# Loops on ScalarE and GpSimd, a shorter loop on VectorE, and the last wo rows loaded in strips

## The chip, the core and the metric

The kernel runs on one core of a Trainium2 chip. The metric is device time in microseconds of one execution, as the median of several. One execution was also taken by the hardware profiler; all rows quoted below come from that one, and times inside it count from the first instruction of its span. A core has five engines with a queue of instructions each: TensorE (PE, matmuls), VectorE (DVE), ScalarE (ACT), GpSimd (POOL) and SyncE (SP, which here only starts transfers). They meet through semaphores. Transfers between HBM (the large memory) and SBUF (the on-chip memory) run on 16 DMA engines that all queues share.

## The reference

One decode step for a batch of two: attention with grouped heads over a long cache, an output projection, a small MLP block on the same layer-normed token, and a gated sum. Cut to what matters:

```python
B, Sq, D = 2, 1, 512
Hq, Hkv, Sk, Dh = 32, 8, 32768, 128
xn = layernorm(x)
q = (xn @ wq)                                   # [B, Hq, 1, Dh]
scores = einsum("bhqd,bhkd->bhqk", q, k) * Dh ** -0.5    # four query heads share one kv head
o = einsum("bhqk,bhkd->bhqd", softmax(scores), v)
s = o.reshape(B, Sq, Hq * Dh) @ wo              # wo is 4096 x 512
out = x + s * silu(mlp_block(xn))               # weights w1 .. w4, hidden width 1792
```

All inputs are bf16. Each of the 2 x 8 pairs of batch and kv head has a K and a V of 32768 x 128, 8 MB each, so the two caches are 268 MB. With S = 1 the shifts inside the MLP block leave nothing of w1 and w2, so the kernel loads w3 and w4 alone.

## The kernel before

There are 16 head groups (one batch entry and one kv head each). For a group, K lands in SBUF with 128 partitions of 64 KB (`kbuf`, three slots of half a K), and V the same (`vbuf`, one V). K is not in the layout that a score matmul wants, so DVE transposes it in 32 x 32 blocks, 16 transposes of 128 x 1024 words a group (L493), through four buffers `T`; PE multiplies them with a padded, head-selecting form of q called `z` (L562) into two PSUM banks `sc`, one for each half. DVE takes the maximum of each half (`peak`, L476), PE spreads it over the partitions (L574), DVE makes `shift` (L503), ACT takes exponentials `ep` with row sums `rs` (L417), DVE transposes these to `pt` (L511) and makes the denominators' input `sm` (L508), and PE multiplies `pt` with V into `o` (L584). ACT copies `o` to `ob` (L420). The rest of a group's head, `head_on` and `head_out` on DVE with `head_oT` and `head_xp` on PE, is worked off inside the next group's K stage; it ends in four columns `oXs`, which POOL copies into `oX` (L438). POOL also writes `z` for the next group (L427).

Order and queues. PE and DVE run loops (PE's body is one group, DVE's two). ACT and POOL have all 16 groups written out one after the other. Every DVE wait in the loop is an instruction of its own (`take`, L473: wait for a semaphore, then subtract), and the DVE loop carries a branch hint at the top of each pass (`hint_back_edge`, L482). SP starts nearly all transfers, in this order: wq, w3, w4, K of group 0, V of group 0 (once the MLP no longer needs `vbuf`), then in turn the next K, when PE reports that the first half of the present K has been used (`s_half`, L398), and the next V, when PE reports that the present V has been used (`s_pv`, L387). The last K and V go in halves (L404, L392). Behind them in the same queue come the seven parts of wo (`wo_parts`, L411): four kv heads at once (2 MB), three heads of 512 KB each, and the last head as 256, 128 and 128 KB, all with 128 partitions. ACT's queue starts the small loads: x, four strips of x into `x4_bf` (L270) and four copies of the MLP's gate g into `g4` (L379).

The end, `pe_output`: PE waits for each wo part (`d_wo`) and for the `oX` columns that go with it, multiplies (L608, L615), and after the last part DVE multiplies by the gate (L520) and adds x (L521), and SP and ACT store one batch row each (L523). PE then runs 24 further waits (`PAD`, L627) and two hinted branches. A semaphore of a transfer counts to 16.

Of the kernel before, what the change touches and what calls it, by code (L numbers as in the profile page):

```python
# [14 lines left out]
DVE = mybir.EngineType.DVE  # L15

KPT = 128
RT = 16
# [74 lines left out]

@with_exitstack
def kernel(
# [62 lines left out]
    rec = sb("rec", [128, rep], F32)  # L158
    on = sb("on", [128, NQ, rep], BF16)
# [4 lines left out]
    x4 = sb("x4", [128, QW], F32)  # L164
# [35 lines left out]
    oX = sb("oX", [128, Hkv, NQ, B], BF16)  # L200
# [11 lines left out]
    wo_parts = [(0, 4, 0, NQ), (4, 5, 0, NQ), (5, 6, 0, NQ), (6, 7, 0, NQ), (7, 8, 0, 2), (7, 8, 2, 3), (7, 8, 3, NQ)]  # L212
    KC = 2
    PAD = 24
# [18 lines left out]
    t_d = sem("t_d")  # L233
    t_k = [sem(f"t_k{i}") for i in range(NPART)]
    t_v = [sem(f"t_v{i}") for i in range(NPART)]
    s_half, s_pv, s_shift, s_oX = (sem(f"s_{n}") for n in ("half", "pv", "shift", "oX"))
# [13 lines left out]
    with tc.tile_critical(sync_engine=mybir.EngineType.Pool, no_gpsimd_drain=True):  # L250
# [5 lines left out]
        nc.sync.sem_inc(t_k[1], 16)  # L256
# [12 lines left out]
        for n in range(NQ):  # L269
            ac.op(lambda e, n=n: e.dma_start(out=x4_bf[32 * n:32 * n + B, :], in_=A_x[:, 0, n * QW:(n + 1) * QW]), e_x4z, inc=(d_x4, 16))  # L270
# [26 lines left out]
        with nc.allow_low_precision(reason="one of the terms is one, the others are zero"):  # L297
# [23 lines left out]
            out=sel_w[:, :, :], in_=row_of[:, :].unsqueeze(1).broadcast_to([128, 4, 32])), e_row)  # L321

# [55 lines left out]
        for n in range(NQ):  # L378
            ac.op(lambda v, n=n: v.dma_start(out=g4[32 * n:32 * n + B, :], in_=g[:, n * QW:(n + 1) * QW]), e_g, e_g0, inc=(d_g, 16))  # L379
        e_x4 = ve.op(lambda v: v.tensor_copy(out=x4[:, :], in_=x4_bf[:, :]), (d_x4, 16 * NQ))  # L380
        ve.op(lambda v: v.memset(qrb[:, :], 0.0), e_qr)
        e_s0 = ve.op(lambda v: v.memset(pro[:, :], 0.0))


        def load_v(m, *events):
            if m < NG - 1:
                sp.op(lambda e: e.dma_start(out=vbuf[:, :], in_=row_view(A_v_cache, *groups[m])), *events, inc=(t_v[0], 16))  # L387
                nc.sync.sem_inc(t_v[1], 16)
                return
            for h in range(NPART):  # L390
                c = slice(h * SLOT, (h + 1) * SLOT)
                sp.op(lambda e, c=c: e.dma_start(out=vbuf[:, c], in_=row_view(A_v_cache, *groups[m])[:, c]), *events, inc=(t_v[h], 16))  # L392

        load_v(0, e_h2)
        for m in range(1, NG):
            base = m % 2
            if m < NG - 1:
# [3 lines left out]
                nc.sync.sem_inc(t_k[1], 16)  # L401
# [7 lines left out]
        for i, (a, c, r0, r1) in enumerate(wo_parts):  # L409
            cols = slice(r0 * D, r1 * D)  # L410
            sp.op(lambda e, a=a, c=c, cols=cols: e.dma_start(out=wo3[:, a:c, cols], in_=wos[:, a:c, cols]), (s_pv, NG - 1), inc=(d_wo[i], 16))  # L411


        for m in range(NG):
            for h in range(NPART):
                i = order(m).index(h)
                ac.op(lambda v, i=i: v.activation(  # L417
                    out=ep[i][:, :], in_=sc[i][:, :], func=ACT.Exp, scale=inv_sqrt_dh, bias=shift[:, :], accum_out=rs[:, i:i + 1]),
                    (s_shift, m + 1), e_tf if m == 0 else None, inc=(t_e, 1))
            ac.op(lambda v: v.copy(out=ob[:, :], in_=o[:, :]), (s_pv, m + 1), inc=(t_ob, 1))  # L420

        z_cols = z[:, :, :, (NR - 1) * rep:].rearrange("p n e c -> p (n e) c")
        z_cols = z_cols[:, :, 0:128].rearrange("p w (j c) -> p w j c", j=4)[:, :, :, 0:rep]

        def put_z(m):
            b, k = groups[m]
            po.op(lambda v: v.tensor_mul(  # L427
                out=z_cols,
                in0=qr[:, :, :, b, k * rep:(k + 1) * rep].rearrange("p n e h -> p (n e) h").unsqueeze(2).broadcast_to([128, 2 * NB, 4, rep]),
                in1=quad[:, :].unsqueeze(1).unsqueeze(3).broadcast_to([128, 2 * NB, 4, rep])),  # L430
                e_qr, e_z0, e_quad, (s_shift, m) if m else None, inc=(t_z, 1))

        e_oX = [None] * NG
        put_z(0)
        for m in range(NG):
            if m:
                b, k = groups[m - 1]
                e_oX[m - 1] = po.op(lambda v, b=b, k=k: v.tensor_copy(out=oX[:, k, :, b], in_=oXs[:, :]), (s_oX, m + 1))  # L438
            if m < NG - 1:
                put_z(m + 1)  # L440


        def head_on(last=False):
            take(nc.vector, t_S)
            nc.vector.tensor_reduce(
                out=den[:, :], in_=S[:, 0:NPART * rep].rearrange("p (i h) -> p h i", h=rep),
                axis=AX.X, op=ALU.add).then_inc(t_d, 1)
            take(nc.vector, t_d)
            nc.vector.reciprocal(out=rec[:, :], in_=den[:, :]).then_inc(t_d, 1)
            take(nc.vector, t_d)  # L450
            nc.vector.tensor_mul(
                out=recm[:, :, :], in0=rec[:, :].unsqueeze(1).broadcast_to([128, NQ, rep]),
                in1=sel_h[:, :].unsqueeze(2).broadcast_to([128, NQ, rep])).then_inc(t_oT, 1)
            take(nc.vector, t_oT, 2)
            ins = nc.vector.tensor_mul(
                out=on[:, :, :], in0=oT[:, :].unsqueeze(1).broadcast_to([128, NQ, rep]), in1=recm[:, :, :])
            if last:
                ins.then_inc(t_on, 1)

        def head_out(last=False):  # L460
            take(nc.vector, t_xp)
            nc.vector.tensor_mul(
                out=xm[:, :, :], in0=xp_b[:, :].rearrange("p (r h) -> p r h", r=NQ),
                in1=mask[:, :].unsqueeze(1).broadcast_to([128, NQ, rep])).then_inc(t_d, 1)
            take(nc.vector, t_d)
            with nc.allow_low_precision(reason="three of the four terms are zero, the fourth is bf16"):
                if last:
                    b, k = groups[-1]
                    return ve.op(lambda v: v.tensor_reduce(out=oX[:, k, :, b], in_=xm[:, :, :], axis=AX.X, op=ALU.add))
                nc.vector.tensor_reduce(out=oXs[:, :], in_=xm[:, :, :], axis=AX.X, op=ALU.add).then_inc(s_oX, 1)  # L470
# [4 lines left out]
        def peak(i):  # L475
            nc.vector.tensor_reduce(out=mx[:, i:i + 1], in_=sc[i][:, :], axis=AX.X, op=ALU.max).then_inc(t_d, 1)  # L476
            take(nc.vector, t_d)
            ins = nc.vector.tensor_scalar_mul(out=mxr[:, i, :], in0=row_of[:, :], scalar1=mx[:, i:i + 1])  # L478
            if i == NPART - 1:
                ins.then_inc(t_mx, 1)  # L480

        with nc.Fori(0, NG // 2, engines=[DVE], hint_back_edge=True):  # L482
            for par in range(2):
                take(nc.vector, t_z)
                for i, h in enumerate(order(par)):
                    take(nc.vector, t_k[i], 16)
                    u = par + h
                    kt = kbuf[:, u * SLOT:(u + 1) * SLOT].bitcast(I32)
                    for r in range(NR):
                        n = i * NR + r  # L490
                        if n >= T_BUFS:
                            take(nc.vector, t_used)
                        nc.vector.transpose(  # L493
                            out=Ts[n % T_BUFS][:, :].rearrange("p (b t k) -> p t b k", b=NB, t=RT),
                            in_=kt[:, r * W:(r + 1) * W].rearrange("p (t b k) -> p t b k", b=NB, t=RT)).then_inc(t_T, 1)
                        if i == 1 and r == 3:
                            peak(0)
                            head_on()
                head_out()
                take(nc.vector, t_used, T_BUFS)  # L500
                peak(1)
                take(nc.vector, t_top)
                nc.vector.tensor_reduce(  # L503
                    out=shift[:, :], in_=S[:, NPART * rep:], axis=AX.X, op=ALU.min).then_inc(s_shift, 1)
                for h in range(NPART):
                    take(nc.vector, t_e)
                    if h == NPART - 1:
                        nc.vector.tensor_mul(  # L508
                            out=sm[:, :, :], in0=sel_h[:, :].unsqueeze(1).broadcast_to([128, NPART, rep]),
                            in1=rs[:, :].unsqueeze(2).broadcast_to([128, NPART, rep]))  # L510
                    nc.vector.transpose(  # L511
                        out=pt[h][:, :, :].rearrange("p r (t h) -> p t r h", h=rep),
                        in_=ep[order(par).index(h)][:, :].rearrange("p (t r h) -> p t r h", r=NR, h=rep)).then_inc(t_pt, 1)
        head_on(last=True)
        e_oX[NG - 1] = head_out(last=True)


        e_ws, e_s = (pe.sem, pe.n + 1), (pe.sem, pe.n + 2)
        e_wsum = ac.op(lambda v: v.copy(out=wsum, in_=qrb[:, :]), e_ws)
        e = ve.op(lambda v: v.tensor_tensor(out=sg[0:QP, :], in0=pro[0:QP, 0:QW], in1=g4[0:QP, :], op=ALU.mult), (d_g, 16 * NQ), e_s)  # L520
        e = ve.op(lambda v: v.tensor_tensor(out=out4[0:QP, :], in0=sg[0:QP, :], in1=x4[0:QP, :], op=ALU.add), e, e_x4)  # L521
        for b, q in ((0, sp), (1, ac)):
            q.op(lambda v, b=b: v.dma_start(out=out[b, 0, :].rearrange("(n c) -> n c", c=QW), in_=out4[b:QP:32, :]), e, inc=(d_out, 16))  # L523
        sp.wait((d_out, 32))


        def head_oT(marks=None):
            take(nc.tensor, t_ob)
            for t in range(VT):
                if t == VT - 1 and marks:  # L530
                    marks.append(nc.tensor.mark_branch_hint_location())
# [18 lines left out]
        with nc.body("pe_groups", valid_engines=[PE]):  # L550
# [39 lines left out]
            ins.then_inc(s_pv, 1)  # L590
# [7 lines left out]
        with nc.body("pe_output", valid_engines=[PE]):  # L598

            marks = [nc.tensor.mark_branch_hint_location()]  # L600
# [63 lines left out]
```

## Time and profile before

| what | value |
|---|---|
| median of 3 runs | 657.68 us (657.57 to 657.85) |
| profiled execution, its own time | 657.31 us |
| its span, first to last instruction | 655.5 us |
| PE, PE weight loads, DVE busy | 409.6, 164.1, 380.2 us |
| ACT, POOL busy | 39.5, 10.1 us |
| bytes moved, mean rate | 280.58 MB, 428 GB/s |
| mean granted clock of TensorE | 0.81 |

The page cuts the span into 40 slices and gives for each the busy share of every engine and of the 16 DMA engines in tenths. The queues are listed with their packets: q1 is what SP starts, q10 what ACT starts, and packets of the kind "instruction" are instruction code that is brought in while the program runs. The chain of waits follows the work that ended last back from the last instruction. A row of the waits names the waiting engine and line, the releaser, the sum in us, the count, and the longest. "DVEq" or "PEq" with L473 means that the engine's own sequencer stood in a `take`.

### The profile page before, as it was taken

The numbers are of one execution on the slowest core, as the hardware profiler recorded it, in microseconds if no ns is written. First come the engines' busy times: TensorE is split into PE (matmuls) and PEld (weight loads), VectorE is DVE, ScalarE is ACT, GpSimd is POOL, SyncE is SP. The second block draws the span as 40 slices with busy tenths as digits, with TensorE's granted clock in tenths as the row PEclk, the third lists the DMA queues.
The fourth block names the chain that finished last, engine by engine and source line by source line (L and its number), as shares of the span: only waits on it lengthen the run. The fifth ranks groups of instructions, "written<-read, shape, count | busy, mean of one in ns | idle before, by whom it ended". The sixth has DMA issues, their size and how long they took to land. (4 is left out here: it accounts for less than half of the span.)

```text
span 655.5 us, 6482 instructions
## 1 busy us (share of the span) xinstructions
PE 409.6 (62%) x2444; PEld 164.1 (25%) x2444; DVE 380.2 (58%) x534; ACT 39.5 (6%) x89; POOL 10.1 (2%) x43
## 2 busy tenths in 40 slices
PE   2528386564938656494765749566383856648765
PEld 0113132231313212131321313232131322213323
DVE  5348194673819457291855729285482937638770
ACT  1100101000010000001000000100001010000100
POOL 1000000000000000000000000000000000000000
PEclk9859677696987769697686969878696887979798
DMA  8999999999999999999999999999999999999996
GB/s 365 435 449 444 445 420 420 444 444 444 396 448 444 444 428 412 448 440 444 416 428 444 440 448 400 444 444 440 440 404 448 440 444 420 424 444 414 448 418 262
DMA packets 6779, 280.58 MB, mean 428 GB/s; under 512 B 746, under 2 KB 1012, under 8 KB 2036
## 3 DMA queue, kind: packets, MB, share of 16 engines
q1 hardware_dynamic: 6728, 280.50, 99.0%
q8 instruction: 2, 0.03, 0.0%
q14 instruction: 5, 0.04, 0.0%
q10 hardware_dynamic: 44, 0.01, 0.0%
HBM read 280.50 MB, written 0.00 MB: 428 GB/s over the span
## 5 line engine op out<-in xcount | busy, mean ns | idle before, releaser
L493 DVE STREAM_TRANSPOSE T<-kbuf 128x1024 int32<-128x1024 int32 x256 | 295.7, 1214 | 186.7 <-DVEq L473 186.4
L562 PE MATMUL sc<-T,z 128*128 128x512 bf16 x1024 | 280.2, 422 | 164.9 <-PEq L473 161.8
L562 PEld LDWEIGHTS sc<-T,z 128*128 128x128 bf16 x1024 | 98.8, 104 | 330.1 <-issue 251.7
L584 PE MATMUL o<-vbuf,pt 128*16 128x512 bf16 x1024 | 90.8, 533 | 35.0 <-PEq L473 35.0
L584 PEld LDWEIGHTS o<-vbuf,pt 128*16 128x16 bf16 x1024 | 34.3, 117 | 85.8 <-issue 78.4
L417 ACT ACTIVATE ep<-sc,shift 128x512 bf16<-128x512 f32 x32 | 21.7, 682 | 479.8 <-DVE shift L503 479.8
L511 DVE STREAM_TRANSPOSE pt<-ep 128x512 bf16<-128x512 bf16 x32 | 22.6, 708 | 15.3 <-DVEq L473 15.3
L476 DVE TENSOR_REDUCE mx<-sc 128x1 f32<-128x512 f32 x32 | 21.5, 672 | 15.7 <-DVEq L473 15.7
L574 PE MATMUL S<-mxr,same_h 128*128 128x64 f32 x32 | 6.5, 284 | 22.0 <-PEq L473 22.0
L532 PEld LDWEIGHTS oT<-sel_o,ob 128*128 128x128 f32 x136 | 17.7, 191 | 3.2 <-issue 0.5
L532 PE MATMUL oT<-sel_o,ob 128*128 128x4 f32 x136 | 16.2, 243 | 0.5 <-PEq L473 0.5
L420 ACT COPY ob<-o 128x512 f32<-128x512 f32 x16 | 9.4, 585 | 97.0 <-PE o L584 97.0
L574 PEld LDWEIGHTS S<-mxr,same_h 128*128 128x128 f32 x32 | 4.8, 188 | 29.8 <-issue 29.8
L438 POOL COPY oX<-oXs 128x4 bf16<-128x4 bf16 x15 | 2.8, 188 | 520.8 <-DVE oXs L470 520.8
L478 DVE TENSOR_SCALAR mxr<-row_of,mx 128x32 f32<-128x32 f32 x32 | 7.7, 241 | 4.8 <-DVEq L473 0.3
L503 DVE TENSOR_REDUCE shift<-S 128x1 f32<-128x64 f32 x16 | 3.6, 225 | 11.2 <-DVEq L473 11.2
L591 PEld LDWEIGHTS S<-sm,ones_f 128*128 128x128 f32 x32 | 4.8, 188 | 6.9 <-issue 6.9
L372 PE MATMUL sc<-vbuf,h_bf 128*2 128x512 bf16 x14 | 4.8, 521 | 2.4 <-DVE h_bf L369 2.4
L417 ACT ACTIVATION_READ_ACCUMULATOR ep<-sc,shift 128x1 f32 x32 | 6.3, 196 | 0.0
L427 POOL TENSOR_TENSOR z<-qr,quad 128x64 bf16<-128x64 bf16 x16 | 4.7, 292 | 102.2 <-DVE shift L503 86.4
L591 PE MATMUL S<-sm,ones_f 128*128 128x8 f32 x32 | 6.2, 266 | 0.0
L336 PE MATMUL sc<-kbuf,xT 128*2 128x512 bf16 x32 | 3.6, 627 | 4.1 <-DMA kbuf<-in_A_wq_dram 4.1
(88 smaller groups left out, 63.6 us busy)
## 6 DMA issues: line engine op xcount, KB each, us to landing
kbuf<-in_A_k_cache_dram SPq DMA_DIRECT2D x2, 4096.0 KB, 21.7
vbuf<-in_A_v_cache_dram SPq DMA_DIRECT2D x2, 4096.0 KB, 20.2
kbuf<-in_A_wq_dram SPq DMA_DIRECT2D x1, 4096.0 KB, 12.3
vbuf<-in_B_w_dram SPq DMA_DIRECT2D x2, 1792.0 KB, 18.0
kbuf<-in_A_wo_dram SPq DMA_DIRECT2D x1, 2048.0 KB, 29.3
kbuf<-in_A_wo_dram SPq DMA_DIRECT2D x3, 512.0 KB, 30.8
kbuf<-in_A_wo_dram SPq DMA_DIRECT2D x1, 256.0 KB, 31.7
kbuf<-in_A_wo_dram SPq DMA_DIRECT2D x2, 128.0 KB, 15.6
```

Source lines behind the costliest of these rows:

```text
L372: e_h2 = pe.op(lambda t, f=f: t.matmul(h2[0:B, :], lhsT=h_bf[:, f * B:(f + 1) * B], rhs=w4v[:, f, :], start=(f == 0), stop=(f == FK - 1)), ...
L417: ac.op(lambda v, i=i: v.activation(out=ep[i][:, :], in_=sc[i][:, :], func=ACT.Exp, scale=inv_sqrt_dh, bias=shift[:, :], accum_out=rs[:, i ...
L420: ac.op(lambda v: v.copy(out=ob[:, :], in_=o[:, :]), (s_pv, m + 1), inc=(t_ob, 1))
L476: nc.vector.tensor_reduce(out=mx[:, i:i + 1], in_=sc[i][:, :], axis=AX.X, op=ALU.max).then_inc(t_d, 1)
L478: ins = nc.vector.tensor_scalar_mul(out=mxr[:, i, :], in0=row_of[:, :], scalar1=mx[:, i:i + 1])
L493: nc.vector.transpose(out=Ts[n % T_BUFS][:, :].rearrange("p (b t k) -> p t b k", b=NB, t=RT), in_=kt[:, r * W:(r + 1) * W].rearrange("p (t ...
L511: nc.vector.transpose(out=pt[h][:, :, :].rearrange("p r (t h) -> p t r h", h=rep), in_=ep[order(par).index(h)][:, :].rearrange("p (t r h) ...
L532: ins = nc.tensor.matmul(oT[:, :], lhsT=ob[:, t * Dh:(t + 1) * Dh], rhs=sel_o[:, t, :], start=(t == 0), stop=(t == VT - 1))
L562: ins = nc.tensor.matmul(sc[i][:, :], lhsT=z[:, nb, w, zc:zc + 128], rhs=Tb[:, nb, :, w], start=(r == 0 and nb == 0 and w == 0), stop=(r = ...
L574: nc.tensor.matmul(S[:, NPART * rep:], lhsT=same_h[:, :], rhs=mxr[:, :, :].rearrange("p i r -> p (i r)"), start=True, stop=True).then_inc( ...
L584: ins = nc.tensor.matmul(o[32 * j:32 * j + VT * rep, :], lhsT=pt[h][:, r, a * VT * rep:(a + 1) * VT * rep], rhs=vt[:, u * VT:(u + 1) * VT, ...
L591: nc.tensor.matmul(S[:, 0:NPART * rep], lhsT=ones_f[:, :], rhs=sm[:, :, :].rearrange("p i h -> p (i h)"), start=True, stop=True).then_inc( ...
```

## The change

- ACT's and POOL's 16 groups become loops (ACT eight passes of two groups, POOL fifteen of one). ACT now waits for DVE's `shift` (`t_shift`) and PE's `o` (`t_pv`) in the loop, and it is ACT that passes "V used" on to SP (`s_pv`). POOL's next `z` waits for `sm` instead of `shift`. A dummy exponential (`warm`) stands ahead of ACT's loop.
- DVE's loop: semaphore waits ride on the instructions that need them and count up through a pass; the subtractions are done together at the end of a pass. The branch hint is placed once, in the prologue, instead of in each pass. In the built program DVE has 147 instructions instead of 192, ACT 40 instead of 80, SP 78 instead of 91, POOL 55 instead of 68.
- Of the seven wo parts the last two (128 KB each) are loaded in strips of 40, 40, 40 and 8 partitions, so SP starts 13 wo transfers instead of 7. Their semaphores count to 64.
- The loads of `x4_bf` and `g4` go to SP's queue; SP's 30 semaphore increments, one at each K and V, become two at the start; the f32 copy `x4` is gone.
- Alignment directives pad the code: DVE's last two operations to slots 126 and 127 of a block of 128 instructions, and what SP, ACT and POOL run after the stores to the start of such a block, PE's end to a block of 256. Padding is jumped over. PE's 24 idle waits are gone; its hinted branch stands ahead of the last wo part.

```diff
+    STRIPS = ((0, 40), (40, 80), (80, 120), (120, 128))
+    wo_rows = [((0, 128),)] * (len(wo_parts) - 2) + [STRIPS] * 2
...
-        nc.sync.sem_inc(t_k[1], 16)
+        nc.sync.sem_inc(t_k[1], 16 * (NG - 1))
+        nc.sync.sem_inc(t_v[1], 16 * (NG - 1))
...
-            ac.op(lambda e, n=n: e.dma_start(out=x4_bf[32 * n:32 * n + B, :], in_=A_x[:, 0, n * QW:(n + 1) * QW]), e_x4z, inc=(d_x4, 16))
+            sp.op(lambda e, n=n: e.dma_start(out=x4_bf[32 * n:32 * n + B, :], in_=A_x[:, 0, n * QW:(n + 1) * QW]), e_x4z, inc=(d_x4, 16))
...
+        hint_v = nc.vector.mark_branch_hint_location()
...
-            sp.op(lambda e, a=a, c=c, cols=cols: e.dma_start(out=wo3[:, a:c, cols], in_=wos[:, a:c, cols]), (s_pv, NG - 1), inc=(d_wo[i], 16))
-        for m in range(NG):
-            for h in range(NPART):
-                i = order(m).index(h)
-                ac.op(lambda v, i=i: v.activation(
-                    out=ep[i][:, :], in_=sc[i][:, :], func=ACT.Exp, scale=inv_sqrt_dh, bias=shift[:, :], accum_out=rs[:, i:i + 1]),
-                    (s_shift, m + 1), e_tf if m == 0 else None, inc=(t_e, 1))
-            ac.op(lambda v: v.copy(out=ob[:, :], in_=o[:, :]), (s_pv, m + 1), inc=(t_ob, 1))
+            for p0, p1 in wo_rows[i]:
+                sp.op(lambda e, a=a, c=c, cols=cols, p0=p0, p1=p1: e.dma_start(
+                    out=wo3[p0:p1, a:c, cols], in_=wos[p0:p1, a:c, cols]), (s_pv, NG - 1), inc=(d_wo[i], 16))
+        with nc.Fori(0, NG // 2, engines=[ACTE]):
+            for par in range(2):
+                take(nc.scalar, t_shift)
...
+                take(nc.scalar, t_pv)
+                nc.scalar.sem_inc(s_pv, 1)
+                nc.scalar.copy(out=ob[:, :], in_=o[:, :]).then_inc(t_ob, 1)
...
+        with nc.Fori(0, NG - 1, engines=[POOL]) as m:
+            put_o(m)
+            take(nc.gpsimd, t_sm)
+            put_z(m + 1)
...
-        with nc.Fori(0, NG // 2, engines=[DVE], hint_back_edge=True):
+        nc.br("dve_groups", engines=[DVE])
+        with nc.body("dve_groups", valid_engines=[DVE]):
+            c = Counts()
...
+            for s_, n in c.totals():
+                take(nc.vector, s_, n)
+            nc.regs_alu(turn_v, turn_v, 1, op=ALU.add)
+            nc.vector.br_lt(turn_v, NG // 2, on_true="dve_groups", on_false="dve_last").branch_hint(hint_v)
...
+        nc.vector.addr_align(128, offset=126, max_nops=0)
...
+            (nc.sync if q is sp else nc.scalar).addr_align(128, max_nops=0)
+        nc.gpsimd.addr_align(128, max_nops=0)
...
+                if i == len(wo_parts) - 2:
+                    nc.tensor.br_ne(turn, 0, "pe_end", "pe_groups").branch_hint(mark)
+                    nc.switch_bb("pe_end")
...
-            for _ in range(PAD):
-                nc.tensor.wait_ge(d_wo[-1], 16)
...
+            nc.tensor.addr_align(256, max_nops=0)
```

## The prediction, made before the result was known

> **What bounds the kernel.** I read the page first, then the waits, then the end of the chain.
>
> ```profile
> DMA  8999999999999999999999999999999999999996
> q1 hardware_dynamic: 6728, 280.50, 99.0%
> q8 instruction: 2, 0.03, 0.0%
> q14 instruction: 5, 0.04, 0.0%
> ```
>
> The DMA engines are full in every slice between the first and the last; SP's queue q1 alone holds them for 99% of the span. The first packet of the weights starts at 1.93 us, the last lands at 651.23, and spread over their durations the packets run at 434 GB/s throughout. A 64 KB packet takes 2418 ns on its engine, a 1 KB packet 46 ns. So only three stretches can move: 1.9 us ahead, the point at which the last of 16 DMA engines is done, and 4.3 us behind that.
>
> The waits, of all engines and then of SP's two kinds of issue, tell how far compute is from mattering:
>
> ```profile
> DVE T L493 <- DVEq L473: 186.4, 39, 12.3
> ACT ep L417 <- DVE shift L503: 479.8, 16, 31.8
> ```
>
> ```profile
> L387 SPq DMA_DIRECT2D vbuf<-in_A_v_cache_dram x15: 327/328/328, 29.2 to 575.7; - x15
> DMA to landing us min/median/max: 24.6/26.4/32.1
> ```
>
> DVE, the busiest engine next to PE, idles up to 12.3 us in one wait for K. A V load (8.39 MB at 434 GB/s: 19.3 us) lands 24.6 us or more after its issue. Less 19.3, the 1.04 us from the first issue (0.89) to its first packet, and 1.7 us by which the slowest DMA engine lands behind the first: 2.6 us in which the next load is queued but not yet needed. A group may grow by that before the stream stops.
>
> The end of the chain (start, us, what) and of the timeline:
>
> ```profile
> 638.62 12.61 DMA kbuf<-in_A_wo_dram
> ...
> 651.27 0.26 PE pro L615 x4
> ...
> 651.55 0.30 DVE sg L520
> ...
> 651.88 0.29 DVE out L521
> ```
>
> The last wo part lands, four matmuls and two DVE operations follow, and the stores go out at 652.19. Their landing at 654.13 and the closing barrier fill the rest.
>
> **Why some DMA engines are late.** Each of the 16 adds one to a transfer's semaphore, so the increments show them finishing. For the last wo part ten come between 649.59 and 649.93, three near 650.16, then 650.60, 651.14 and 651.23. The three late ones were made long before: after an instruction packet at 35.84 one engine falls back 0.85 us, after one at 71.86 (16 KB, q8) another 1.4, after 265.30 a third 0.6, after 638.05 a fourth 0.5, and they never catch up, since each engine has its own share of every load. Inside the window 649 to 652:
>
> ```profile
> q8 instruction: 1, 0.02, 2.0%
> q14 instruction: 1, 0.01, 0.6%
> ```
>
> Two more; the q14 packet at 650.54 puts 0.31 us on the second-latest engine (650.50 for the part before, 651.14 instead of 650.83). The trace does not name who asked for a packet. By time, 35.84 fits DVE entering its loop (31.8), 71.86 and 649.70 PE (the only 16 KB ones), 265.30 ACT, 638.05 POOL, 643.37 SP, 650.54 DVE leaving its loop.
>
> **Part by part.**
>
> *Loops on ACT and POOL, fewer SP instructions.* With half the code on ACT and 13 instructions less on POOL and SP, the packets at 265.30, 638.05 and 643.37 should go; their three engines (at most 650.60) were not last: 0 by itself, up to -0.1. New costs: the word "V used" passes through ACT, a wait and an increment. A DVE wait instruction delays the next operation by 0.11 us (57.13 to 57.24), so I take 0.2; the 2.6 us hide it. `z` waits for `sm`, 1.85 us later than `shift` (609.68 against 607.83), so the last `z` comes at 610.0 instead of 608.14; DVE's next transposes start at 612.24. ACT's branch runs in idle stretches of up to 31.8 us. At the end `ob` comes 0.2 later, so `oX` at 648.6 instead of 648.43; the part that needs it is multiplied at 650.63: hidden, and bare only if wo came 2 us sooner.
>
> *DVE's loop.* About 40 wait instructions a pass go, ten subtractions come at its end, 10 x 0.11 = 1.1 us beside the wait for K. 0 in the stream. The early hint may keep the packet at 35.84 away: its engine is the second-latest, so this matters only together with the latest.
>
> *x4 and g on SP.* Eight issues of 0.33 us each, ahead of V 0 (29.2) and between V 0 and K 1 (53.39), where SP waits over 20 us; they are read at 651.55. 0. On their two DMA engines 27 ns rows lie in line instead of on a second queue: 0 to -0.1.
>
> *Strips.* The two parts are 256 rows of 1 KB. Loads over 2 partitions show data packets on two engines, stores over 4 on four, loads over 128 on all 16: an even split over a divisor. For 40 partitions the largest up to 16 is 10 engines with 4 rows each; for 8 it is 8. Three strips of 40 and one of 8 give, for both parts, 26 rows on eight engines, 24 on two, none on six, instead of 16 everywhere. Ten engines gain 10 x 46 ns = 0.46 us and six semaphore packets of 9 ns (0.05); six lose 16 x 46 = 0.74. Ordinary engines then end at 650.1 to 650.45. The latest (0.96 to 1.4 us behind; I keep the q8 packet at 71.86, as PE's loop is unchanged) ends at 651.23 - 0.74 = 650.49 if it is one of the six, at 651.74 if one of the ten. Which engines the six are no row shows; I take the first, because nothing late is known of the two that carry x and g, and because the sizes fit (0.5 + 0.74 against 1.4). [...]
>
> *Issues.* Eight strips instead of two: 8 x 0.45 = 3.6 us from 638.6 on, when the queue takes them (before that it stalls SP for 13.4 and 6.3 us). They are issued by 642.3; wo part 4, ahead of them, lands from 648.9: 6 us of cover. [...]
>
> *Alignment.* Jumps on SP and ACT come after the stores have been issued, POOL's after `out4`: beside the 1.3 us in which SP waits for the stores. Between +2.8 (a late fetch, below) and -0.2 (no packet beside the stores); nearest is the covered case, 0.
>
> **Sum.** Last landing 650.5 instead of 651.23, the 4.3 us behind it unchanged: -0.7. Span 654.8, profiled time 656.6. The median shown is 0.37 above the profiled execution, so 657.68 - 0.7 = 657.0.
>
> **Rivals.**
> - *The latest engine is one of the ten.* Last landing 651.74: +0.5, 658.2. For it: ten of sixteen. Against: fewer late engines remain.
> - *The strips do nothing:* 40 partitions go over all 16, or the queue shares otherwise. Then only packets saved count: 651.23 stays, 657.7, or 657.3 if the packet at 71.86 moves. The 2- and 4-row transfers speak against it.
> - *Slower: the jump at the end lands in code that is not there.* SP's jump over the padding is the place. From DVE's loop entry (31.7) to its packet (35.84) are 4.1 us under load; if SP must wait that long, 1.3 are covered and 2.8 bare: 657.0 + 2.8 = 659.8. It decides once the fetch takes over 1.3 + 0.7 = 2.0 us. Idle DMA engines speak for 1.4 (1.04 issue to packet, 0.31 packet). [...] This trace's back edges show no packet between 71.86 and 638 but one, so the loops are held to be free here.
>
> **Chances.** The forecast 0.64 (656.3 to 657.4 mostly; 0.16 of it, with every packet gone and a shorter end, beats 656.4); latest engine among the ten 0.12; strips without effect 0.08; late fetch or another stall 0.16. A difference under 0.2% (1.3 us) is about what a measurement of this kernel cannot tell from none. So faster 0.16, slower 0.16 and the rest, 0.68, within. Range 656.0 (all 16 engines level, at 650.07, is -1.2; some tenths from the stores) to 658.7 (latest among the ten, with half a microsecond more at the end); the late fetch lies outside.
>
> **What would show it.** Right: no q14 packets between 264 and 267 and around 638 and 643; the last part's increments within some 0.4 us; DVE's last product (then L573) starting near 650.8; SP's issue of the stores near 651.5. Wrong: the last increment beyond 651.2; the six engines late by more than 1.3; SP idle after the stores' landing; instruction packets recurring every pass, each of which would put its engine back by 0.3 to 0.9 us.

## The result, and the profile after

| what | before | after |
|---|---|---|
| median (lowest to highest), 13 executions each | 657.66 us (657.19 to 657.87) | 659.08 us (658.55 to 659.51) |
| ratio, 95% interval | | 1.0023 (1.0015 to 1.0031) |
| profiled execution, its span | 657.31, 655.5 us | 659.23, 657.3 us |
| last completion of a wo part | 651.23 us | 652.20 us |
| stores issued, landed | 652.19, 654.13 us | 653.21, 655.91 us |

The change costs 1.4 us, 0.23%. Forecast were 657.0 us and, at 0.68, a difference under 0.2%; both missed, and the time lies above the range (656.0 to 658.7).

The page of the changed kernel (busy share of the DMA engines in 40 slices, then the queues):

```profile
DMA  8999999999999999999989999899999999999995
q1 hardware_dynamic: 6804, 280.50, 98.8%
q8 instruction: 3, 0.05, 0.0%
q14 instruction: 6, 0.05, 0.0%
```

Its waits (engine, line, releaser, sum, count, longest):

```profile
ACT ep L458 <- ACTq L449: 486.8, 16, 33.4
...
DVE T L534 <- DMA kbuf<-in_A_k_cache_dram: 191.0, 17, 14.4
```

Its V loads as SP issues them:

```profile
L417 SPq DMA_DIRECT2D vbuf<-in_A_v_cache_dram x15: 327/328/356, 30.3 to 577.2; - x15
...
DMA to landing us min/median/max: 25.8/27.1/29.9
```

The middle of the program is as before: DMA engines full, compute waiting for K (DVE's longest wait 14.4 us, before 12.3), a V load landing 25.8 us or more after its issue (before 24.6). Nothing of the 1.4 us is compute. The end of its chain (start, us, what) moved as a block:

```profile
617.87 33.73 DMA kbuf<-in_A_wo_dram
...
652.24 0.31 PE pro L670 x4
...
652.57 0.30 DVE sg L573
...
652.89 0.29 DVE out L574
```

And the timeline at the stores, before and after:

```profile
652.19 0.64 SPq L523 DMA_DIRECT2D out_dram<-out  x1
652.20 0.60 ACTq L523 DMA_DIRECT2D out_dram<-out  x1
```

```profile
653.21 0.61 SPq L576 DMA_DIRECT2D out_dram<-out  x1
653.22 0.61 ACTq L576 DMA_DIRECT2D out_dram<-out  x1
```

The stores land 1.78 us later, and the span is longer by as much: the last wo completion (the increment by which a DMA engine reports its share of a transfer) comes 0.97 later (652.20), the stores are issued 1.01 behind it instead of 0.96 (+0.05), and they land 2.70 us after issue instead of 1.94 (+0.76). Of the 0.97, about 0.5 is older: the median completion of the last V half comes at 640.37 instead of 639.84, as between 98 and 216 us the 64 KB packets of many engines at once took longer, six times, and cost 0.03 to 0.22 us each. That belongs in part to this one execution (below).

### The profile page after: what moved, and what is told of

It is laid out like the page before. It is cut to its first block, busy times and chain, and to the rows that moved or that the text cites. A ratio compares the mean times of both kernels' runs of the same rounds, so it can differ in the third digit from the quotient of the medians.

```text
span 657.3 us, 6262 instructions
## 1 busy us (share of the span) xinstructions
PE 399.5 (61%) x2412; PEld 162.7 (25%) x2444; DVE 378.6 (58%) x533; ACT 39.7 (6%) x90; POOL 10.3 (2%) x44
## 5 line engine op out<-in xcount | busy, mean ns | idle before, releaser
L617 PE MATMUL sc<-T,z 128*128 128x512 bf16 x992 | 273.7, 422 | 181.3 <-PEq L449 177.0
L639 PE MATMUL o<-vbuf,pt 128*16 128x512 bf16 x1024 | 84.8, 504 | 33.5 <-PEq L449 33.5
L639 PEld LDWEIGHTS o<-vbuf,pt 128*16 128x16 bf16 x1024 | 31.7, 111 | 80.7 <-issue 70.2
L478 POOL COPY oX<-oXs 128x4 bf16 (+1 forms) x16 | 3.0, 188 | 541.6 <-POOLq L449 541.6
L491 DVE TENSOR_REDUCE den<-S 128x4 f32<-128x8 f32 x17 | 2.7, 159 | 5.7 <-PE S L646 5.7
```

The costliest lines, as they stand in the source:

```text
L617: ins = nc.tensor.matmul(sc[i][:, :], lhsT=z[:, nb, w, zc:zc + 128], rhs=Tb[:, nb, :, w], start=(r == 0 and nb == 0 and w == 0), stop=(r = ...
L639: ins = nc.tensor.matmul(o[32 * j:32 * j + VT * rep, :], lhsT=pt[h][:, r, a * VT * rep:(a + 1) * VT * rep], rhs=vt[:, u * VT:(u + 1) * VT, ...
```

## The experiments

Each kernel is compared with the kernel before on the same chip; the medians of that one lie between 657.34 and 657.66 us. A ratio's interval is some 0.0009 to either side, 0.6 us. All edits are of the changed kernel, where nothing else is said, and are shortened.

**1. The change without strips.**

```diff
-    wo_rows = [((0, 128),)] * (len(wo_parts) - 2) + [STRIPS] * 2
+    wo_rows = [((0, 128),)] * len(wo_parts)
```

> The changed kernel with the last two wo parts as one load of 128 partitions each, all else kept. Theory A (the ten engines that carry the strips end late, because each strip adds a completion to every engine, and the increments come up to 1.2 us behind the last packet instead of 0.3): the one late engine is then the last again, at about 651.9 to 652.2 in the profile, against 652.20 with strips, so -0.3 to 0 us against the changed kernel, 658.8 to 659.1. Rival B (the strips work as forecast and the loss is elsewhere): the late engine gains its 16 rows back, +0.7 us, 659.8. Rival C (the strips are the whole loss): -1.4 us, 657.7.

Measured: 658.47 us (658.20 to 658.72), ratio 1.0015 (1.0006 to 1.0024). The last wo completion is at 651.14, as in the kernel before, and yet the time is 0.9 us longer. It lies between A (658.8) and C (657.7). So the strips are some 0.5 of the 1.4 us, and the rest is behind the last load.

**2. The strips alone, on the kernel before** (13 wo transfers instead of 7, semaphores to 64).

> The kernel before, with the last two wo parts in strips of 40, 40, 40 and 8 partitions, and nothing else. Theory A (completions pile up on the ten engines): the increments of the last part on these ten come up to 1 us behind their packets, last landing about 651.5 instead of 651.23, +0.2 to +0.5 us, 657.9 to 658.2. Rival B (the split works and the late engines are among the six that carry no strip): last landing 650.5, -0.7 us, 657.0. Rival C (the late engines are among the ten): 651.7 and more, +0.5 us.

Measured: 658.40 us, ratio 1.0013 (1.0004 to 1.0021), last completion 652.38 us. By themselves the strips lose time. Rival C is out as well: the latest engine ends with part 4 at 651.13, after all completions of part 5 (651.06), so it carries no strip.

**3. Without any alignment, with strips and without.**

```diff
-        nc.vector.addr_align(128, offset=126, max_nops=0)
-            (nc.sync if q is sp else nc.scalar).addr_align(128, max_nops=0)
-        nc.gpsimd.addr_align(128, max_nops=0)
-            nc.tensor.addr_align(256, max_nops=0)
```

> The changed kernel without the five alignment directives (VectorE, SyncE, ScalarE, GpSimd, TensorE), all else kept. Theory A (jumping over the padding brings code in while the stores land, and TensorE's last branch waits 3.5 us for its block): TensorE's last branch back to 0.1 us, stores landing 1.9 us after their issue instead of 2.7, so -0.8 us, 658.3. Rival B (the end is late because of the strips' many completions, not the code): stores still land 2.7 us after their issue, 0 us, 659.1. Rival C (code brought in earlier now puts an engine back inside the stream): the stores are quick, but the last wo part lands 0.3 to 0.8 us later, 658.6 to 659.1.

> The changed kernel without strips and without alignment: the loops, the fused waits and the moved small loads alone. Theory A (the loops as such are free, and the 0.65 us by which the whole stream ran late in the profile of the changed kernel is that execution's own): -0.8 to -1.2 us against the changed kernel, 657.9 to 658.3, that is 0.2 to 0.6 above the kernel before. Rival B (the loops slow the stream itself by 0.65 us each time): the median arrival of the last V part is again 0.6 to 0.7 us later than in the kernel before. Rival C (fewer instruction packets help as forecast): 0.3 us or more below the kernel before.

Measured: 661.15 us with strips (five executions, 659.39 to 661.51) and 659.97 without (657.71 to 660.88). The span fell to 655.5 us without strips, and the stores land 1.9 us after issue again. But the time outside the span, 1.7 to 2.3 us in all other kernels, is 2.0 to 5.2 us, another in each execution. In the two traces a 16 KB instruction packet on q8 (PE's by its times, experiment 4) starts 2.5 and 1.8 us after the span's end. Most kernels with the old PE end have such a packet too, 1.1 to 1.6 us after it, so the packet alone does not make the difference. That the end waits for a fetch of PE's last code is inferred: the trace has no instruction there. Experiment 4 shows that it hangs on PE's end.

**4. Whose alignment: PE's end as in the kernel before, or PE's alignment alone, or all others alone** (none of the three has strips).

```diff
# first: no alignment; PE's end as before (the hint of the changed kernel goes, two come back)
-                if i == len(wo_parts) - 2:
-                    nc.tensor.br_ne(turn, 0, "pe_end", "pe_groups").branch_hint(mark)
...
+            marks = [nc.tensor.mark_branch_hint_location()]
+            head_oT(marks)
...
+            for _ in range(24):
+                nc.tensor.wait_ge(d_wo[-1], 16 * len(wo_rows[-1]))
+            for n, mark in enumerate(marks):
+                nc.tensor.br_ne(turn, 0, f"pe_output_{n}", "pe_groups").branch_hint(mark)
+                nc.switch_bb(f"pe_output_{n}")
# second: only nc.tensor.addr_align(256, max_nops=0)
# third: PE's end as in the first, alignment on DVE, SP, ACT and POOL
```

> The changed kernel without strips and without any alignment, but with PE's end as in the kernel before (two branch hints, 24 idle waits, two hinted branches). Theory 1: without alignment the program only lacked the fetch of PE's last code, which the old end brings in early, and the loops cost nothing. Then the stores land 1.9 us after their issue (654.1), the span is 655.4 us, the stretch outside the span is back to 1.8 or 1.9 us, and the time is 657.3 us (ratio 0.999 to 1.000). Rival: the long stretch outside the span (2.0 to 5.2 us without alignment) belongs to the loops or to another engine's code; then the span is 655.5 and the time stays at 659 to 660.5 us.

> The changed kernel without strips, with the alignment of PE's end alone (those of DVE, SP, ACT and POOL left out). Theory 1: it is the jumps of SP, ACT and POOL whose fetches put the stores back; without them the stores land 1.9 us after issue, at 654.1, and PE's jump of 3.5 us from 651.2 on is the last to end, at 654.75; span 656.0, time 657.9. Rival: PE's own fetch of 16 KB beside the stores puts them back; then they land 2.7 us after issue as before, span 656.5, time 658.4.

> The changed kernel without strips, with the alignments of DVE, SP, ACT and POOL, but PE's end as in the kernel before. Theory 1 (fetches of SP, ACT and POOL beside the stores): the stores land 2.7 us after issue, at 654.9 to 655.1; span 656.3, time 658.2. Rival (PE's fetch was it): stores within 1.9 us, span 655.5, time 657.4.

| kernel without strips | time us | span of the profiled execution | stores land after issue | PE's jump |
|---|---|---|---|---|
| old PE end, no alignment | 657.52 | 655.9 | 1.91 | none |
| PE's alignment alone | 657.96 | 656.1 | 1.92 | 3.39 |
| the others' alignment alone | 658.17 | 656.5 | 2.60 | none |
| both (experiment 1) | 658.47 | 656.5 | 2.93 | 3.55 |

Theory 1 gave 657.3, 657.9 and 658.2. The transfers of the changed kernel without strips, then of the one with the old PE end, between 653 and 656 us, where the stores go (eight packets each on q1 and q10):

```profile
DMA  0000000200000000330000000000000008000000
...
q14 instruction: 3, 0.02, 2.3%
q8 instruction: 1, 0.02, 2.1%
q1 hardware_dynamic: 8, 0.00, 0.3%
q10 hardware_dynamic: 8, 0.00, 0.2%
```

```profile
DMA  0000000000000000000000000000000000000000
...
q10 hardware_dynamic: 8, 0.00, 0.2%
q1 hardware_dynamic: 8, 0.00, 0.2%
```

SP and ACT jump over their padding at 652.81 in the first; 1.4 us later, at 654.25 and 654.28, two 8 KB packets run, and two of the stores' ten increments come at 654.88 and 655.09 while the rest are in by 654.22. With PE's alignment alone there is no q14 packet there and no late increment. The others' alignments were not tried one by one, DVE's among them. PE's own jump is 3.4 to 3.6 us whenever it is aligned (a packet of 16 KB starts 1.0 us after it and takes 1.0 to 1.1 us); alone it ends at 654.67, 0.5 us behind the stores. In every row of the table, and before and after, the span ends 1.4 us behind the later of the two, the stores' landing or the end of PE's jump. With both alignments that is the stores (655.09 against 654.74; in the changed kernel 655.91 against 655.73): PE's jump is then hidden, and the late stores cost the 0.9 us.

The first row is also the answer on the loops, the shorter DVE loop and the moved issues: 657.52 us, ratio 0.9997 (0.9988 to 1.0006). Within that interval they cost nothing and bring nothing.

**5. The change without its alignment** (strips of 40, 40, 40 and 8, old PE end; three executions profiled).

> The changed kernel with its strips of 40, 40, 40 and 8, without alignment, with PE's end as in the kernel before: the change without its alignment part. Theory 2 (an engine's completions of small transfers come in one after the other, some 0.18 us each, and pile up): data packets of wo end by 650.6, the last completion lands at 651.9 to 652.3; time 657.52 + 0.6 to 0.9 = 658.1 to 658.4. Theory 3 beside it (bursts of slower 64 KB packets come with the strips): 0.2 to 0.8 us of excess over 2418 ns in the stream. Rival (strips cost only beside the alignment's jumps): last landing 651.5, time 657.5.

> The kernel with the strips of 40, 40, 40 and 8 and the old PE end, looked at again. Theory 3b (in most executions of it the 64 KB packets run long somewhere): excess over 2418 ns of 0.3 to 1.0 us, the last completion later by as much, span 656.0 to 656.7. Theory 2 (late completions at the end): no excess, last completion at 651.7 to 652.3, span 656.0 to 656.7. An execution like the first (no excess, last completion 651.3, span 655.6) tells nothing.

> The same kernel, a third look, with the same two expectations: excess of 0.3 to 1.0 us in the stream, or none and a last completion at 651.7 to 652.3; span 656.0 to 656.7 in both.

Measured: 658.13 us (657.53 to 658.68), ratio 1.0009 (1.0000 to 1.0018). The profiled execution and the two more came to 657.90, 657.22 and 657.79 us, with last completions at 651.32, 651.13 and 651.55. None is as late as 651.7, so the expected pile-up is smaller than theory 2 said. It is there: the last 1 KB packet ends at 650.38, 650.15 and 650.58, 0.94 to 0.97 us before the last completion; with single loads (experiment 1) that is 0.32. The third has about a quarter of a microsecond more in long 64 KB packets than the other two.

**6. Two strips a part (88 and 40), and three parts cut so.**

```diff
+    wo_rows = [((0, 128),)] * (len(wo_parts) - 2) + [((0, 88), (88, 128))] * 2      # four strips in all
+    wo_rows = [((0, 128),)] * (len(wo_parts) - 3) + [((0, 104), (104, 128))] + [((0, 88), (88, 128))] * 2
```

> As the run with the old PE end, with the last two wo parts in two strips of 88 and 40 partitions instead of one load: by divisors 11 engines with 8 rows and 10 with 4, so 12 rows on ten engines, 8 on one, none on five, and at most two completions an engine and part instead of four. Theory 2 (uneven rows do relieve the late engine, what cost time was the number of small transfers, whose completions come in late): the late engine, if it is one of the five, last lands at 650.4, the ten at 650.3; span 654.7, time 656.6. If the late engine is one of the ten, its last landing is 651.5 and the time 657.7. Rival (any split delays the completions): last landing 651.8 or later although the data packets end by 650.5, time 658 or more.

> As the run with two strips of 88 and 40 on the last two parts, with the part before them (2 KB rows) in strips of 104 and 24 as well: 10 rows on twelve engines, 8 on one, none on three. If the late engine is one of the three, its last landing moves from 651.26 to the one of part 3 (650.6) and the ordinary engines' from 650.77 to 650.95; less bursts in the stream, both are lower. Theory: time 657.0 to 657.4, below both kernels. Rival: the late engine is the one with 8 rows or one of the twelve, and lands at 651.3 to 651.5: time 657.8 to 658.0, no gain.

Measured: 657.88 us, ratio 1.0004 (0.9995 to 1.0013), and 658.80 us, ratio 1.0019 (1.0010 to 1.0028). In the first the mechanism of the forecast is plain: the late engine finishes with part 4 at 651.26 and takes no part in the last two, whose completions are all in by 650.77, 0.5 before it. Against the 0.73 us that this saves the engine stand 0.4 us by long 64 KB packets, and 0.5 us by which its part 4 is late in all kernels with uneven strips (next section). In the second 1 KB packets took up to 125 ns instead of 46, and most executions were 0.7 us longer than the profiled one; that expectation failed, and why is open.

**7. Even strips: four of 32 adjacent partitions, or each spread by a step of 4** (old PE end; 16 rows on every engine as with one load).

```diff
+    wo_rows = [((0, 128),)] * (len(wo_parts) - 2) + [((0, 32), (32, 64), (64, 96), (96, 128))] * 2
+    wo_rows = [((0, 128),)] * (len(wo_parts) - 2) + [((0, 128, 4), (1, 128, 4), (2, 128, 4), (3, 128, 4))] * 2
```

> As the run with the old PE end, with the last two wo parts in four even strips of 32 partitions each: 16 rows on every engine as in one load, but eight completions an engine for the two parts instead of two. Theory 2 (the number of small transfers): completions pile up, the 14 or 15 ordinary engines' last ones come at 650.4 to 650.8 instead of 649.9, the last of all at 652 or later; time 658.0 to 658.4. Rival (it was the uneven rows, with ten engines at 26): ordinary completions within 0.1 us of 649.9, last landing 651.1 to 651.5, time 657.5.

> As the run with even strips (four of 32 partitions, 658.69 us), but each strip takes every fourth partition from 0, 1, 2 or 3 on, so that it is spread over all 128. Rows per engine and the number of completions are the same. Theory 2a (number of small transfers): nothing changes, ordinary engines' last completions at 650.4 to 651.3, the last of all at 652.4, time 658.7. Theory 2b (a strip of adjacent partitions is written at half the rate): the pile-up goes, ordinary engines end at 649.9 to 650.0, the last of all at 651.1 to 651.6 as with single loads, time 657.5.

Measured: 658.69 us, ratio 1.0017 (1.0008 to 1.0026), and 658.15 us, ratio 1.0011 (1.0002 to 1.0020), against 657.52 us with single loads. Neither pure theory holds. Spread, all 1 KB packets take 46 ns again, but the late engine still reports its last eight completions about 0.155 us apart (650.46, 650.62, ... 651.55), though two rows are 92 ns. From its part 4 to its end it takes 1.26 us instead of 0.73; the median is 0.6 us longer. Adjacent partitions add 0.5: 1 KB packets take up to 86 ns, and the late engine's 2 KB packets, still of part 4, up to 265 instead of 84, so that its part 4 is in at 651.18 instead of 650.29. PE's 16 KB packet falls into the same stretch in both (649.81 and 649.57); how much of this one delay is its work is open.

**8. Even strips of adjacent partitions on parts 1 and 2 (512 KB each).**

> As the run with the old PE end, with four even strips of 32 partitions on wo parts 1 and 2 (512 KB each), where their completions are not last; the last parts are single loads. It has as many transfers as the changed kernel. Theory 3 (bursts of slower 64 KB packets in the stream come with more transfers or with SP's longer code): 0.2 to 0.8 us of excess over 2418 ns between 60 and 260 us, and the time is 657.8 to 658.3. Rival (the bursts come by chance, or the strips cost by late completions alone): excess under 0.05 us, time 657.5.

Measured: 660.41 us, ratio 1.0042 (1.0028 to 1.0055): a cost of 2.9 us that neither theory expected, and no long 64 KB packets. The transfers of this kernel between 640 and 653 us, then of the one with single loads:

```profile
DMA  9999999999999999999999999999998999971100
GB/s 391 391 441 416 403 429 429 416 416 429 416 416 429 416 429 214 277 240 202 202 214 227 252 227 265 240 240 265 302 353 296 347 369 337 350 221 50 47 19 25
```

```profile
DMA  9999999999999999999999999999730010000000
GB/s 403 391 429 429 429 403 403 429 441 416 416 429 416 416 441 429 403 403 429 416 429 416 416 422 378 391 397 356 252 104 22 25 32 3 0 0 0 0 0 0
```

While the strips run (slices 16 to 28) the engines are as busy as ever but move 202 to 277 GB/s instead of 391 to 441; 4 KB packets take up to 478 ns instead of 159. So strips of 32 adjacent partitions were written here at little more than half the rate of loads over 128. The trace does not show why.

**9. The changed kernel's strips, spread by a step of 3** (40, 40, 40 partitions over all of 0 to 119, then 8), with the old PE end and in the changed kernel as it is.

```diff
+    STRIPS = ((0, 120, 3), (1, 120, 3), (2, 120, 3), (120, 128))
```

> As the run with the strips of 40, 40, 40 and 8 and the old PE end (658.13 us), but the strips of 40 take every third partition from 0, 1 or 2 on. Rows per engine stay 26, 24 and none. Theory 2b: the completions follow the packets by 0.3 us, ten engines end at 650.5 to 650.8, the late one (if among the six) at 650.3 to 651.0 with the part ahead; time 656.9 to 657.3, below the 657.52 of single loads. Theory 2a: nothing changes, time 658.1.

> The changed kernel as it is (659.08 us), with its strips of 40 spread by a step of 3 and nothing else changed. Theory 2b: it comes to the 658.47 us of the changed kernel without strips, or up to 0.5 us below it since the late engine is relieved: 658.0 to 658.4. Theory 2a: 659.1.

Measured: 658.67 us (657.43 to 659.43), ratio 1.0013 (1.0004 to 1.0022), and 658.63 us (658.42 to 660.07), ratio 1.0020 (1.0010 to 1.0030). The first was meant to beat both kernels and does not: four of eleven executions lie at 657.4 to 657.6, the others at 658.1 to 659.4, and the profiled one (657.43, last completion 651.26) is of the lower group. What the upper group does is open. The second lies between its two theories (658.0 to 658.4, and 659.1). So no gain from spreading these strips of 40 is shown; with adjacent partitions (experiment 5) all their 1 KB packets take 46 ns already.

**10. SP's code as long as with strips, without strips** (14 further semaphore increments behind the last wo issue, old PE end).

> As the run with the old PE end and single loads (657.52 us), with 14 further semaphore increments on SP behind its last wo issue, so that SP's code is as long as with the strips. Theory 4 (the length of SP's code brings the packet): a q14 packet of 8 KB between 640 and 650 us, one more DMA engine 0.3 to 0.4 us late, the last landing up to 0.4 later, time 657.5 to 657.9. Rival (the strips' transfers bring it): no q14 packet there, time 657.5.

Measured: 657.75 us, ratio 1.0003 (0.9994 to 1.0012). Instruction queues between 643 and 650 us in this kernel, with the longer code:

```profile
q8 instruction: 1, 0.02, 0.9%
q14 instruction: 1, 0.01, 0.3%
```

and without it:

```profile
q8 instruction: 1, 0.02, 0.9%
```

The longer code on SP brings the packet (at 644.81 here). So the strips' six further transfers should bring theirs by their length: 646.94 in the changed kernel, 646.4 to 646.5 in experiment 5. Without alignment, the kernels with single loads and those with 9 or 10 wo transfers have no q14 packet while wo loads.

## Why the prediction was wrong

Measured: +1.4 us where -0.7 was forecast. Point by point:

- **The bound, the loops, x4 and g, SP's increments: right.** The packets at 35.84, 265.30, 638.05 and 643.37 are gone (one at 646.94 is new), the V loads keep their lead, and the parts together are 0.9997 of the time before. The loops' back edges show no packet behind the one at 69 to 72 us.
- **The split of the strips: right.** The last part's semaphore gets 38 increments from transfers, three times 10 and 8. The late engine was one of the six, as taken: its last completion is that of part 4 (651.60 in the changed kernel, 650.90 in the cleanest execution of experiment 5). The counts bear out the split taken from the transfers over 2, 4 and 128 partitions: 10 engines for 40 partitions, 8 for 8. That every strip takes the same ten engines, so that they carry 26 or 24 rows and six carry none, was the author's estimate; no run shows it as a whole. In its place the runs show that the late engine carries no strip, and that the engine that ends last has eight completions, one for each strip.
- **"Ordinary engines then end at 650.1 to 650.45": the first step that failed.** In the cleanest execution the ten end at 651.13, so that 651.23 becomes 651.13 and not 650.49. How the end is reached, from packets and increments (us):

| execution | part 4: latest engine | second latest | last 1 KB packet ends | last of the last part |
|---|---|---|---|---|
| before | 650.49 | 650.17 | 650.91 | 651.23 |
| change without strips (1) | 650.41 | 649.24 | 650.82 | 651.14 |
| the same, old PE end, no alignment (4) | 650.31 | 649.30 | 650.92 | 651.52 |
| changed kernel | 651.60 | 650.47 | 651.03 | 652.20 |
| strips, old PE end (5) | 650.94 | 649.80 | 650.38 | 651.32 |
| the same again | 650.90 | 649.60 | 650.15 | 651.13 |
| strips spread, old PE end (9) | 650.94 | 650.01 | 650.33 | 651.26 |

With single loads the end is the latest engine's part 4 plus 0.73 or 0.74, its 16 rows of 46 ns. Only in experiments 4 (old PE end) and 10 another engine comes later, 1.2 us behind, which fits PE's 16 KB packet at 649.53 and 649.99.

With strips the latest engine drops out. Counted back from the last completion, the engine that ends last has eight completions some 0.19 us apart, and its part 4 before them: that of the second latest in experiment 5 and in the changed kernel, that of the third latest (649.72) in experiment 9. It is 1.52 or 1.53 us in all, in the changed kernel 1.73, with the 0.31 us packet at 650.52. The data were in time: the last 1 KB packet ends at 650.15 in the cleanest execution, and with the usual 0.3 us to a completion that is about what was forecast. The completions were not. The term that was mis-sized is "six semaphore packets of 9 ns (0.05)". Completions come some 0.19 us apart behind four rows (184 ns of data) and behind a single row (46 ns) alike, so the two strips of 8 partitions cost an engine 0.29 us more than their data. The ten pay 0.8 us (1.53 less 0.73) where the sum had 0.51. Why completions keep this distance is not shown. Adjacent partitions are not the reason for these strips: spread by a step of 3 they have the same distance and the same 1.53 us.

Two more things eat the gain. The second latest engine is later with strips, at 649.60 to 650.02 where single loads without the packet have 649.24 to 649.40; that fits the packet that SP's longer code brings (649.76 in experiment 10, with single loads; but 649.38 in experiment 7's spread strips, which have the packet too). And the latest engine did not gain its whole 0.74: its part 4 comes 2.38 to 2.43 us behind its part 2 in all nine profiled executions with uneven strips on the last two parts alone, 1.84 or 1.85 with single loads. Why these 0.55 us are lost is open.

- **The other rivals.** The latest engine is not one of the ten, and the strips do have an effect, so both fall; the time of the second (657.3 to 657.7) is nevertheless about what experiment 5 gives in its three profiled executions, since gain and cost cancel there.
- **What a further transfer costs.** The sum charged it 9 ns on its engine. In the kernel before, the last two parts, single loads of 128 KB, land 0.33 us apart (650.90 and 651.23), no more than their eight rows of 46 ns. Smaller transfers cost more than their packets (experiment 7, spread): about 0.155 us on the late engine for a transfer of 32 KB with 92 ns of data, so that 16 rows of 1 KB take 1.26 us in eight transfers instead of 0.73 in two.
- **"Alignment ... nearest is the covered case, 0": the second step that failed, and the larger.** It cost 0.9 to 1.0 us. The rival named a jump at the end into code that is not there, gave it 0.16, and put it on SP at 2.8 us. A late fetch was the right kind of cause, its place and price were wrong: PE's jump takes 3.5 us (3.49 in the changed kernel, where it is hidden; alone +0.4), and with the others' alignment instruction packets run beside the stores, two of whose increments come 0.4 to 0.9 us behind the rest (alone +0.65). That these packets are what delays them is argued from the times; that this alignment does it is shown. "Beside the 1.3 us in which SP waits for the stores" took the wait for a cover; what was hidden in it delayed the thing waited for. The loops cost nothing of the kind: no packet comes at their back edges behind the one at 69 to 72 us, and with them alone the time is 0.9997 of the one before (experiment 4). Why they differ from PE's jump is not shown.
- **"PE's 24 idle waits are gone" was priced at nothing.** In the changed kernel PE's alignment stands in their place, so this is no part of the 1.4 us. Without the old end and without alignment the time is 2.4 us longer (experiments 3 and 4, 659.97 against 657.52). The waits and the second hint were put back together, so which of them does it is not shown. An early fetch fits: with the old end a 16 KB packet comes on q8 at 648.5 to 651.7, while wo loads, and without it there is none.
- **What stays open.** The 64 KB packets ran long by 0.2 to 0.8 us in a profiled execution in five of thirteen executions with strips and in one of seven without, so the strips are not shown to cause it; nor is it known how much of the changed kernel's median it makes. The upper group of experiment 9 and the longer executions of experiment 6 have no trace. The shares of the 1.4 us are therefore: 0.9 to 1.0 alignment (shown), some 0.5 with the strips (shown by the difference, with an interval as large). In the three profiled executions of experiment 5 the loads end where single loads end (651.13 to 651.55), and all three are faster than its median (657.22 to 657.90 against 658.13). So the traces show why the strips gain nothing, and not why the median with them is longer.

## What to carry to other kernels

A step that is hidden behind a wait is free only if it doesn't use what the wait is for: here instruction packets ran in the wait for two stores, on the 16 DMA engines that serve these too, and the stores landed 2.60 to 2.93 us after issue instead of 1.91. Code at the end of this program was paid for by its place (0.9 to 1.0 us for the alignment), and an idle stretch of instructions may have been doing work (2.4 us more without PE's old end); take such a stretch out alone first. Before relieving one late DMA engine, look at the second latest, and count what the relief itself adds: completions (here some 0.19 us apart, even for one row), code (an 8 KB packet, 0.31 us on its engine), and the range of partitions that each piece covers (202 to 277 GB/s for 32 adjacent ones, 391 to 441 for 128).

## What the runs showed of the hardware that was not expected

- Loads to 32 adjacent partitions moved 202 to 277 GB/s with all engines busy, those to 128 moved 391 to 441 (experiment 8).
- An engine's completions of two-row transfers came about 0.155 us apart, 92 ns of data notwithstanding (experiment 7, spread); those of strips with four rows and with one came some 0.19 us apart, both (experiment 5 and the changed kernel).
- Inside the span, instruction packets were 16 KB on q8 (0.96 to 1.18 us each in the kernels before and after) and 8 KB on q14 (0.31 to 0.51 us); q14's came 1.3 to 1.5 us after a jump on SP or ACT, and PE stood 3.4 to 3.6 us in its jump.
- Six further transfers, or 14 further increments, on SP brought one 8 KB packet into the last loads (646.94 in the changed kernel, 644.81 in experiment 10).
